# A GeGLU feed-forward kernel by seven-product blocks: one plain tile at the head instead of two, seventeen gate products before the first half of x

## The chip, the cores and the metric

The kernel runs on one core of one Trainium2 chip. The metric is the device time of one execution in microseconds (us). Nine runs of the kernel before lie between 274.5 and 275.85 us, with a median of 275.36 us.

## What is computed

```python
B, S, D, F = 32, 32, 1024, 3584        # 1024 tokens
def reference(x, w_gate, w_up, w_down):
    return (_gelu(x @ w_gate) * (x @ w_up)) @ w_down    # all bf16, gelu with tanh
```

## The kernel before, in words

**Two layers.** The first layer makes g = gelu(x·w_gate)·(x·w_up), transposed, in 28 tiles of 128 columns of F (FT = 28). The second multiplies g by w_down and stores the result. The change touches the first layer only, above all its first 30 us.

**Seven products instead of eight.** For one tile of F, the two weight matrices and the two halves of D (rows of x transposed) and of the tokens form a 2x2 by 2x2 block product. The blocks of weights are a11 and a12 (gate, front and rear half of D) and a21 and a22 (up, front and rear). The blocks of x are b11, b21 (tokens 0 to 511, front and rear half of D) and b12, b22 (tokens 512 to 1023). Each block product is KD = 4 matmuls of 128x128 by 128x512. Done plainly a tile takes eight of them for its two matrices and two halves of the tokens (32 matmuls). Done by the Strassen-Winograd scheme it takes seven (28 matmuls), at the price of sums of blocks:

- sums of weights, one set for each tile: s1 = a21 + a22, s2 = s1 - a11, s4 = a12 - s2, s3 = a11 - a21 (`sums`, lines 161 to 171; they are made for a chunk of two tiles at once);
- sums of x, made once: t1 = b12 - b11 (L331), t2 = b22 - t1 (L336), t3 = b22 - b12 (L379), t4 = b21 - t2 (L381), and the copy b22r of b22 (L337).

The seven products are P1 = a11·b11 and P2 = a12·b21, which are in bf16, and s1·t1, s2·t2, s4·b22, s3·t3 and a22·t4, whose operands are 32 bits wide (fp32r).

**Chunks and the loop.** Tiles go in chunks of FC = 2. The two tiles of chunk 0 are done plainly while x and its sums are not there yet (`plain`, L250 to L258, for both halves of the tokens). The loop at L387 handles chunks 1 to 13. For the tiles of one chunk, TensorE does s1·t1 into a bank `psc`, which ScalarE copies out (`sn5`), then s2·t2 on top of P1 in `psa` (copied out as `sn2`), then the last product a22·t4 of the chunk before, then s4·b22 on top of `psc`. VectorE adds `sn2` and `psc` (`added`, L348 to L351), and ScalarE makes `h1` = gelu of that and then the copy `a22r` (L177), which is the last read of that tile's up-weights. Then come P2, where it is still to be made, P1 of the next chunk (`first_product`, L358), and s3·t3.

**P2 ahead.** P2 needs only b21, the quarter of x that is loaded first. For the first NAHEAD = 10 tiles after chunk 0 (tiles 2 to 11) it is made ahead (`product_ahead`, L283) from `a12_ahead`, loaded as three groups of KB = 4, 4 and 2 tiles, and copied to `ahead` by ScalarE and VectorE. `first_product` adds it to P1 later (a read of `psa` and of `ahead` on VectorE).

**Who makes the sums of weights.** VectorE makes them for chunk 1, GpSimd for chunks 2 to 13, one chunk before they are used. At L383 a copy of one column of t4 into `ident` on GpSimd holds GpSimd's queue until t4 is there:

```python
        begun = [first_product(FC + fl, p1[fl]) for fl in range(FC)]
        tt(t3, b22, b12, SUB)
        next(chunk1)
        tt(t4, b21, t2, SUB)
        nc.gpsimd.tensor_copy(ident[:, :1], t4[:, 0, :1])
```

**Order and buffers.** The schedule is manual: each engine runs its instructions in the order in which the program names them, and waits on semaphores. Nearly all loads are issued from SyncE's queue in the order written. x comes through DMA transposes (`load_xT`), apart from the first quarter of b21, which TensorE transposes. Eight PSUM banks have tags: A has four, B two and C two; a bank is given out again in turn (`acc`, L104). Up-weights have two buffers (`wu`), gate-weights three (`wg`).

Of the kernel before, what the change touches and what calls it, by code (L numbers as in the profile page):

```python
# [13 lines left out]
def kernel(  # L14
# [20 lines left out]
    nc = tc.nc  # L35
    P = nc.NUM_PARTITIONS
    fp32 = mybir.dt.float32
# [9 lines left out]
    NB = 512  # L47
# [4 lines left out]
    NCH = FT // FC  # L52
    NAHEAD = 10
# [21 lines left out]

    def g_tiles(name, dtype, cols):

        return [
            gpool.tile(
                [P, k1 - k0, cols],  # L80
                dtype,
                name=name,
                tag=f"{name[:2]}{k1 - k0}",
                bufs=2,
            )
            for k0, k1 in batches
        ]

    g_lo = g_tiles("lo", bf16, N)

    def by_batch(tiles):
        def at(k):
            b = next(i for i, (k0, k1) in enumerate(batches) if k < k1)
            return tiles[b][:, k - batches[b][0], :]

        return at

    def g_of(ft):
        k = ft % HF
        return by_batch(g_lo if ft < HF else g_hi)(k)  # L100
# [15 lines left out]
    def x_rows(dt, nb):  # L116
        return ((b11, b12), (b21, b22))[dt // KD][nb][:, dt % KD, :]


    ahead = [  # L120
        gpool.tile([P, n, NB], fp32, name="ahead", tag=f"hi{n}", bufs=2) for n in (KB, KB, QF - KB)
    ]
    assert 2 * KB < NAHEAD <= KB + QF
# [7 lines left out]
    def load_w(eng, ci, which, d0, d1):  # L131
        f0 = ci * FC * P
        src = (wg_r, wu_r)[which]
        eng.dma_start(out=w_tiles[ci, which][:, d0:d1, :], in_=src[:, d0:d1, f0 : f0 + FC * P])

    def load_w_all(ci, which):

        alloc_w(ci, which)
        if ci < NCH - 2:
            load_w(nc.sync, ci, which, 0, KD if which == 0 and is_ahead(ci) else DT)  # L140
            return


        for d0 in (0, KD):
            load_w(nc.sync, ci, which, d0, d0 + KD)

    def is_ahead(ci):
        return 0 < ci and (ci + 1) * FC <= FC + NAHEAD

    def quads(ci, fl=None):  # L150
        cols = slice(None) if fl is None else slice(fl * P, (fl + 1) * P)
        wg, wu = w_tiles[ci, 0], w_tiles[ci, 1]
        a12 = wg[:, KD:, cols]
        if is_ahead(ci):
            i, j = divmod((ci - 1) * FC, KB)
            a12 = a12_ahead[i][:, :, j * P : (j + FC) * P][:, :, cols]
        return wg[:, :KD, cols], a12, wu[:, :KD, cols], wu[:, KD:, cols]
# [3 lines left out]
    def sums(ci, eng):  # L161

        a11, a12, a21, a22 = quads(ci)
        s1, s2, s4, s3 = (
            spool.tile([P, KD, FC * P], f32r, name=n, tag=n) for n in ("s1", "s2", "s4", "s3")
        )
        s_tiles[ci] = (s1, s2, s3, s4)
        yield eng.tensor_tensor(s1, a21, a22, ADD)  # L168
        yield eng.tensor_tensor(s2, s1, a11, SUB)  # L169
        yield eng.tensor_tensor(s4, a12, s2, SUB)  # L170
        yield eng.tensor_tensor(s3, a11, a21, SUB)  # L171

    a22rs = {}

    def a22r_of(ft):
        t = spool.tile([P, KD, P], f32r, name="a22r", tag="a22r", bufs=2)
        nc.scalar.copy(t, quads(*divmod(ft, FC))[3])  # L177
        a22rs[ft] = t
# [10 lines left out]
    with tc.manual_schedule():  # L189
# [12 lines left out]
        def load_ahead(i, k0, k1, eng=nc.sync):  # L202
            f0, n = FC + i * KB, min(KB, NAHEAD - i * KB)
            eng.dma_start(
                out=a12_ahead[i][:, k0:k1, : n * P],
                in_=wg_r[:, KD + k0 : KD + k1, f0 * P : (f0 + n) * P],
            )

        def load_w0(eng, d0, d1):
            for which in (0, 1):  # L210
                load_w(eng, 0, which, d0, d1)
# [10 lines left out]
        for which, eng in enumerate((nc.sync, nc.scalar)):  # L222
            load_w(eng, 0, which, KD, KD + KQ)
        load_xT(0, KD + KQ, DT)
        load_ahead(0, KQ, KD)
        load_w0(nc.sync, KD + KQ, DT)
        load_ahead(1, 0, KD)
        load_xT(0, 0, KD)
        load_w0(nc.sync, 0, KD)
        load_xT(1, 0, KD)  # L230
        load_xT(1, KD, DT)

# [17 lines left out]
        def plain(ps, which, fl, nb, d0, d1, first=0, last=DT - 1):  # L250
            for dt in range(d0, d1):
                nc.tensor.matmul(  # L252
                    ps,
                    lhsT=w_tiles[0, which][:, dt, fl * P : (fl + 1) * P],
                    rhs=x_rows(dt, nb),
                    start=(dt == first),
                    stop=(dt == last),
                )  # L258
# [6 lines left out]
        def plain_out(ft, nb, h, up):  # L265
            tt(g_of(ft)[:, nb * NB : (nb + 1) * NB], h, up, MUL)
# [12 lines left out]
        def ahead_of(ft):  # L279
            i, j = divmod(ft - FC, KB)  # L280
            return ahead[i][:, j, :]

# [10 lines left out]


        ps = [acc(t) for t in "CCAA"]

        def plain0(tok0, d0, d1):
            for which in (0, 1):
                for dt in range(d0, d1):
                    for fl in range(FC):  # L300
                        plain(tok0[fl][which], which, fl, 0, dt, dt + 1, KD, KD - 1)
# [9 lines left out]
        tok0 = [(acc("A"), acc("B")) for _ in range(FC)]  # L311
        plain0(tok0, KD, KD + KQ)
        for j, copy in enumerate((nc.scalar.copy, nc.vector.tensor_copy) * 2):
            product_ahead(ps[j], 0, j, KQ)
            copy(ahead[0][:, j, :], ps[j])
        plain0(tok0, KD + KQ, DT)
        a12_ahead.append(xpool.tile([P, KD, (NAHEAD - 2 * KB) * P], bf16, name="a12b"))
        load_w_all(1, 1)
        load_w_all(1, 0)
        load_ahead(2, 0, KD)  # L320
        load_w_all(2, 0)
        for j, tag in enumerate("CCAA"):
            ps = acc(tag)
            product_ahead(ps, 1, j)
            (nc.scalar.copy, nc.vector.tensor_copy)[j % 2](ahead[1][:, j, :], ps)
        for fl in range(FC):
            for which in (0, 1):
                plain(tok0[fl][which], which, fl, 0, 0, KD, KD, KD - 1)
            plain_out(fl, 0, gelu(tok0[fl][0], "h0", 4), tok0[fl][1])
            if fl == 0:  # L330
                tt(t1, b12, b11, SUB)  # L331
        tok1 = [(acc("A"), acc("B")) for _ in range(FC)]
        for fl in range(FC):
            for which in (0, 1):
                plain(tok1[fl][which], which, fl, 1, 0, KD)
        tt(t2, b22, t1, SUB)  # L336
        nc.scalar.copy(b22r, b22)  # L337
        chunk1 = sums(1, nc.vector)
        for _ in range(3):
            next(chunk1)  # L340
        for fl in range(FC):
            for which in (0, 1):
                plain(tok1[fl][which], which, fl, 1, KD, DT)
            tok1[fl] = gelu(tok1[fl][0], "h0", 4), tok1[fl][1]
        load_w_all(2, 1)
# [12 lines left out]
        def first_product(ft, psa=None):  # L358
            if psa is None:
                psa = acc("A")  # L360
                prod(psa, quads(*divmod(ft, FC))[0], b11, True)
            if ft < FC + NAHEAD:
                return psa, gelu(added(ahead_of(ft), psa), "h0", 4)
            return psa, snap(psa, "sn1")
# [6 lines left out]
        p1 = [acc("A") for _ in range(FC)]  # L371
        for fl in range(FC):
            prod(p1[fl], quads(1, fl)[0], b11, True)
        for j, tag in enumerate("CC"):
            ps = acc(tag)
            product_ahead(ps, 2, j)
            nc.scalar.copy(ahead[2][:, j, :], ps)  # L377
        begun = [first_product(FC + fl, p1[fl]) for fl in range(FC)]
        tt(t3, b22, b12, SUB)  # L379
        next(chunk1)  # L380
        tt(t4, b21, t2, SUB)  # L381

        nc.gpsimd.tensor_copy(ident[:, :1], t4[:, 0, :1])  # L383
        for fl in range(FC):
            plain_out(fl, 1, *tok1[fl])
        open_fts = []
        for ci in range(1, NCH):  # L387
            fts = range(ci * FC, (ci + 1) * FC)
            if fts[0] == HF:
                g_hi = g_tiles("hi", bf16, N)  # L390
# [5 lines left out]
            s1, s2, s3, s4 = ([s[:, :, fl * P : (fl + 1) * P] for fl in range(FC)] for s in s_tiles[ci])  # L396
# [3 lines left out]
            for fl in range(FC):  # L400
                prod(psc[fl], s1[fl], t1, True)
                sn5.append(snap(psc[fl], "sn5"))
            for fl in range(FC):
                prod(psa[fl], s2[fl], t2, False)
                sn2.append(snap(psa[fl], "sn2"))
# [9 lines left out]
            if fts[0] < FC + NAHEAD:  # L415
                h0 = first
            else:
                for fl in range(FC):
                    psb = acc("B")
                    prod(psb, quads(ci, fl)[1], b21, True)  # L420
                    h0.append(gelu(added(first[fl], psb), "h0", 4))
            begun = [first_product(ft + FC) for ft in fts] if ci + 1 < NCH else []
# [193 lines left out]
```

## Time and profile before

| what | value |
|---|---|
| median of nine runs | 275.36 us (274.5 to 275.85) |
| profiled execution, its own time | 275.64 us |
| span of that execution | 273.9 us |
| TensorE (PE) busy | 268.8 us, 98% of the span |
| VectorE (DVE), ScalarE (ACT), GpSimd (POOL) busy | 195.5, 111.1, 107.4 us |
| read from HBM | 29.62 MB |

Times below are microseconds from the span's start. In a timeline a row gives the start, the time taken, the engine, the line of the kernel, the operation, output<-input with the shapes, and in brackets the idle time of the engine before it with what ended it. PEld is TensorE's weight load, which overlaps its matmuls; SPq is SyncE's queue of DMA issues. A matmul's row lasts longer than the distance to the next, since matmuls are pipelined.

### The profile page before, as it was taken

The numbers are of one execution on the slowest core, as the hardware profiler recorded it, in microseconds if no ns is written. First come the engines' busy times: TensorE is split into PE (matmuls) and PEld (weight loads), VectorE is DVE, ScalarE is ACT, GpSimd is POOL, SyncE is SP. The second block draws the span as 40 slices with busy tenths as digits, with TensorE's granted clock in tenths as the row PEclk, the third lists the DMA queues.
The fourth block names the chain that finished last, engine by engine and source line by source line (L and its number), as shares of the span: only waits on it lengthen the run. The fifth ranks groups of instructions, "written<-read, shape, count | busy, mean of one in ns | idle before, by whom it ended". The sixth has DMA issues, their size and how long they took to land.

```text
span 273.9 us, 3350 instructions
## 1 busy us (share of the span) xinstructions
PE 268.8 (98%) x1190; PEld 189.4 (69%) x1206; DVE 195.5 (71%) x196; ACT 111.1 (41%) x181; POOL 107.4 (39%) x55
## 2 busy tenths in 40 slices
PE   8999999999999999999999999999999999999995
PEld 4444677877778676776868686755447888888883
DVE  1259996879856676766666556568989999999611
ACT  1162654543653646455553636430200032962001
POOL 1000099998797794949576675000000000000000
PEclk9999999999999999999999999999999999999999
DMA  7993412404505415050504280003992245786202
GB/s 193 283 246 86 115 54 61 117 26 130 151 6 152 125 31 154 0 153 0 156 20 134 71 273 4 0 2 112 352 333 87 78 145 199 245 262 223 78 0 78
DMA packets 53841, 33.77 MB, mean 123 GB/s; under 512 B 9792, under 2 KB 53824, under 8 KB 53824
## 3 DMA queue, kind: packets, MB, share of 16 engines
q1 hardware_dynamic: 50304, 31.00, 38.7%
q10 hardware_dynamic: 3520, 2.56, 2.9%
q8 instruction: 9, 0.15, 0.3%
q14 instruction: 8, 0.07, 0.1%
HBM read 29.62 MB, written 2.10 MB: 116 GB/s over the span
## 4 chain that ended last, share of the span: by engine, by line
PE 98%; issue 0%; ACT 0%; DVE 0%
PE psA L270 34%; PE psA L446 18%; PE psC L270 17%; PE psC L446 7%; PE psB L446 7%; PE psB L270 5%; PE psB L252 3%; PE psA L252 2%; PE psC L285 2%; PE psA L285 1%; PE psA L235 1%; PE tp L243 0%; ACT o_sb L586 0%; DVE b L246 0%
## 5 line engine op out<-in xcount | busy, mean ns | idle before, releaser
L270 PE MATMUL psA<-t,s 128*128 128x512 f32 x208 | 54.1, 402 | 0.0
L262 ACT ACTIVATE h<-c 128x512 bf16<-128x512 f32 x52 | 31.6, 627 | 36.9 <-DVE c L350 36.9
L270 PEld LDWEIGHTS psA<-t,s 128*128 128x128 f32 x208 | 39.1, 188 | 9.2
L168 POOL TENSOR_TENSOR s<-wu 128x1024 fp32r<-128x1024 bf16 x12 | 26.5, 2206 | 25.0 <-DMA wu<-in_w_up_dram 21.5
L350 DVE TENSOR_TENSOR c<-sn,psA 128x512 f32<-128x512 f32 x26 | 17.8, 683 | 16.7 <-PE psA L270 16.7
L270 PEld LDWEIGHTS <-wg 128*128 128x128 bf16 x168 | 15.4, 98 | 20.1 <-issue 3.4
L169 POOL TENSOR_TENSOR s<-s,wg 128x1024 fp32r<-128x1024 f32 x12 | 27.8, 2314 | 0.9
L171 POOL TENSOR_TENSOR s<-wg,wu 128x1024 fp32r<-128x1024 bf16 x12 | 26.6, 2213 | 0.0
L355 ACT COPY sn<-psA 128x512 f32<-128x512 f32 x42 | 23.6, 585 | 7.0 <-PE psA L270 6.9
L270 PE MATMUL psA<-t,a22r 128*128 128x512 f32 x104 | 25.9, 391 | 0.0
L270 PE MATMUL psC<-t,s 128*128 128x512 f32 x104 | 25.8, 390 | 0.0
L355 ACT COPY sn<-psC 128x512 f32<-128x512 f32 x26 | 15.2, 589 | 26.2 <-PE psC L270 22.4
L270 PE MATMUL psC<-b22r,s 128*128 128x512 f32 x104 | 25.7, 389 | 0.0
L270 PE MATMUL psA<-b,wg 128*128 128x512 bf16 x100 | 24.1, 379 | 0.2
L270 PEld LDWEIGHTS psC<-t,s 128*128 128x128 f32 x104 | 19.4, 188 | 4.4 <-ACT ahead L377 0.3
L270 PEld LDWEIGHTS psA<-t,a22r 128*128 128x128 f32 x104 | 19.5, 188 | 4.1
L270 PEld LDWEIGHTS psC<-b22r,s 128*128 128x128 f32 x104 | 19.5, 188 | 4.0
L350 DVE TENSOR_TENSOR c<-sn,psC 128x512 f32<-128x512 f32 x26 | 17.6, 686 | 5.0 <-PE psC L270 5.0
L369 DVE TENSOR_TENSOR hi<-h,psA 128x512 bf16<-128x512 bf16 x14 | 9.6, 688 | 14.6 <-PE psA L270 14.6
L425 DVE TENSOR_TENSOR lo<-c,h 128x512 bf16<-128x512 f32 x12 | 19.2, 1597 | 0.6
L170 POOL TENSOR_TENSOR s<-wg,s 128x1024 fp32r<-128x1024 bf16 x8 | 17.3, 2158 | 0.6
L489 ACT COPY snb<-psC 128x512 f32<-128x512 f32 x4 | 2.1, 589 | 36.5 <-PE psC L446 36.5
(94 smaller groups left out, 412.3 us busy)
## 6 DMA issues: line engine op xcount, KB each, us to landing
wdb<-in_w_down_dram SPq DMA_DIRECT2D x12, 512.0 KB, 4.8
wu<-in_w_up_dram SPq DMA_DIRECT2D x11, 512.0 KB, 3.9
wdb<-in_w_down_dram SPq DMA_DIRECT2D x12, 384.0 KB, 4.7
wg<-in_w_gate_dram SPq DMA_DIRECT2D x6, 512.0 KB, 5.1
wg<-in_w_gate_dram SPq DMA_DIRECT2D x10, 256.0 KB, 4.3
v<-in_w_down_dram SPq DMA_DIRECT2D x4, 512.0 KB, 7.6
out_dram<-o_sb ACTq DMA_DIRECT2D x16, 128.0 KB, 1.7
v<-in_w_down_dram SPq DMA_DIRECT2D x4, 384.0 KB, 7.9
```

The source lines that it names most:

```text
L168: yield eng.tensor_tensor(s1, a21, a22, ADD)
L169: yield eng.tensor_tensor(s2, s1, a11, SUB)
L170: yield eng.tensor_tensor(s4, a12, s2, SUB)
L171: yield eng.tensor_tensor(s3, a11, a21, SUB)
L252: nc.tensor.matmul(ps, lhsT=w_tiles[0, which][:, dt, fl * P : (fl + 1) * P], rhs=x_rows(dt, nb), start=(dt == first), stop=(dt == last),)
L262: nc.scalar.activation(h, src, ACT.Gelu_apprx_tanh)
L270: nc.tensor.matmul(ps, lhsT=lhs[:, k, :], rhs=rhs[:, k, :], start=(start and k == 0), stop=(k == KD - 1), skip_group_check=True,)
L350: tt(t, s, ps, ADD)
L355: nc.scalar.copy(t, ps)
L369: tt(g_of(ft)[:, :NB], h0, psa, MUL)
L425: tt(g_of(ft)[:, NB:], added(sn5[fl], psa[fl]), h1[fl], MUL)
L446: nc.tensor.matmul(banks[m], lhsT=lhs(k)[:, m * P : (m + 1) * P], rhs=rhs(k), start=(start and k == 0), stop=(k == HF - 1), skip_group_che ...
```

## The change

- **Chunks.** Only tile 0 is done plainly. Chunk 0 of the loop is now tile 1 alone, done by seven products; chunks 1 to 13 are as before. NCH stays 14.
- **P2 ahead.** 17 tiles instead of 10: tile 1 (from chunk 0's own weights) and four full groups, tiles 2 to 17. The last two groups lie in buffers of `s2` and `s4` that are reused later, so the a12 weights of tiles 10 to 17 are loaded a second time with their chunk (`a12_stays` is true for tiles 2 to 9 only).
- **Loads.** The four groups and all of chunk 0's weights come before b11, b12 and b22.
- **Order at the head.** Groups 1, 2 and 3 of P2 ahead, then tile 0's front half for tokens 0 to 511, its front half for the other tokens, P1 of tile 1, and tile 0's rear half for the other tokens. VectorE makes the sums of chunk 0 (128x512 each) ahead of t1; GpSimd makes those of chunks 1 to 13.
- **The hold on GpSimd** is on t2 instead of t4, and stands before t4.
- Buffers of `ahead` and of g are shared in another way, and of all later loads of weights only the last chunk's gate-weights still come in two halves (before: gate and up of the last two chunks).

```diff
+    chunks = [range(1, FC)] + [range(f0, f0 + FC) for f0 in range(FC, FT, FC)]
+    NCH = len(chunks)
+    NAHEAD = 17
...
-        if ci < NCH - 2:
-            load_w(nc.sync, ci, which, 0, KD if which == 0 and is_ahead(ci) else DT)
+        if (ci, which) != (NCH - 1, 0):
+            load_w(nc.sync, ci, which, 0, KD if which == 0 and a12_stays(ci) else DT)
...
+        a12_ahead += [spool.tile([P, KD, KB * P], bf16, name="a12b", tag=t) for t in ("s2", "s4")]
         load_xT(0, KD + KQ, DT)
         load_ahead(0, KQ, KD)
         load_w0(nc.sync, KD + KQ, DT)
-        load_ahead(1, 0, KD)
+        for i in (1, 2):
+            load_ahead(i, 0, KQ)
+            load_ahead(i, KQ, KD)
+        load_w0(nc.sync, 0, KD)
+        load_ahead(3, 0, KD)
         load_xT(0, 0, KD)
-        load_w0(nc.sync, 0, KD)
         load_xT(1, 0, KD)
         load_xT(1, KD, DT)
+        for which in (1, 0):
+            load_w_all(1, which)
...
+        both = (nc.scalar.copy, nc.vector.tensor_copy)
+        tok0 = (acc("B"), acc("B"))
+        p2_1 = acc("A")
...
+        rear0(KD, KD + KQ)
+        for j in range(KB):
             product_ahead(ps[j], 0, j, KQ)
...
+        rear0(KD + KQ, DT)
+        nc.scalar.copy(ahead_at[0], p2_1)
+        group_ahead(1, "CCAA", both)
+        group_ahead(2, "CCAA", both)
+        for _ in sums(0, nc.vector):
+            pass
+        group_ahead(3, "CCAA")
+        for which in (0, 1):
+            plain(tok0[which], which, 0, 0, KD, KD, KD - 1)
+        tt(t1, b12, b11, SUB)
+        plain_out(0, gelu(tok0[0], "h0", 4), tok0[1])
+        tok1 = (acc("C"), acc("A"))
+        for which in (0, 1):
+            plain(tok1[which], which, 1, 0, KD)
+        p1 = acc("A")
+        prod(p1, quads(0, 0)[0], b11, True)
+        for which in (0, 1):
+            plain(tok1[which], which, 1, KD, DT)
+        nc.scalar.copy(b22r, b22)
         tt(t2, b22, t1, SUB)
...
+        begun = [first_product(1, p1)]
+        tok1 = gelu(tok1[0], "h0", 4), tok1[1]
         tt(t3, b22, b12, SUB)
-        next(chunk1)
+
+        nc.gpsimd.tensor_copy(ident[:, :1], t2[:, 0, :1])
         tt(t4, b21, t2, SUB)
-
-        nc.gpsimd.tensor_copy(ident[:, :1], t4[:, 0, :1])
-        for fl in range(FC):
-            plain_out(fl, 1, *tok1[fl])
+        plain_out(1, *tok1)
         open_fts = []
-        for ci in range(1, NCH):
-            fts = range(ci * FC, (ci + 1) * FC)
+        for ci in range(NCH):
+            fts = chunks[ci]
```

In the changed kernel `rear0` does, for the given quarter of D, tile 0's gate and up matmuls for tokens 0 to 511 and tile 1's P2; `group_ahead(i, ...)` does the four products of group i and copies them out.

## The prediction

> **What bounds the kernel now.** The first page says it at once: TensorE is busy nearly all the time, and the chain that ended last is TensorE.
>
> ```profile
> PE 268.8 (98%) x1190; PEld 189.4 (69%) x1206; DVE 195.5 (71%) x196; ACT 111.1 (41%) x181; POOL 107.4 (39%) x55
> ...
> PE 98%; issue 0%; ACT 0%; DVE 0%
> ```
>
> So time comes only from fewer matmuls or from a wait of TensorE, and in the stage that is changed there is none to win: the chain of waits in order of time runs from 4.1 us on without a gap over 0.07 us. It also gives the price of a matmul:
>
> ```profile
> 24.72 0.86 PE psA L252 x4
> ...
> 31.82 1.81 PE psA L270 x8
> ```
>
> A bf16 matmul of 512 columns takes 0.216 us (0.865/4), one with 32-bit operands 0.227 (1.814/8). I then read VectorE's timeline from 28 to 37 us and GpSimd's whole one, since the change moves what these two do there.
>
> ```profile
> 28.81 2.29 DVE L379 TENSOR_TENSOR t<-b,b 128x2048 fp32r<-128x2048 bf16 x1
> 31.02 1.22 DVE L171 TENSOR_TENSOR s<-wg,wu 128x1024 fp32r<-128x1024 bf16 x1
> 32.15 2.29 DVE L381 TENSOR_TENSOR t<-b,t 128x2048 fp32r<-128x2048 bf16 x1
> ```
>
> ```profile
> 34.60 0.19 POOL L383 CAST ident<-t 128x1 bf16<-128x1 f32 x1 [33.30 <-PE psC L270]
> 34.81 2.13 POOL L168 TENSOR_TENSOR s<-wu 128x1024 fp32r<-128x1024 bf16 x1
> ```
>
> Up to 34.4 us VectorE makes t1 to t4 and four sums with GpSimd idle: each 128x2048 step starts 2.2 us before the next. GpSimd's first sum begins 0.37 us after t4's end (34.44). What happens when both work is seen later, in VectorE's timeline and in GpSimd's at the same moment:
>
> ```profile
> 60.60 2.51 DVE L425 TENSOR_TENSOR lo<-c,h 128x512 bf16<-128x512 f32 x1
> 63.04 0.67 DVE L350 TENSOR_TENSOR c<-sn,psA 128x512 f32<-128x512 f32 x1
> 63.75 2.67 DVE L425 TENSOR_TENSOR lo<-c,h 128x512 bf16<-128x512 f32 x1
> ```
>
> ```profile
> 60.41 2.16 POOL L171 TENSOR_TENSOR s<-wg,wu 128x1024 fp32r<-128x1024 bf16 x1
> 63.72 2.14 POOL L168 TENSOR_TENSOR s<-wu 128x1024 fp32r<-128x1024 bf16 x1 [1.15 <-DMA wu<-in_w_up_dram]
> 65.94 2.48 POOL L169 TENSOR_TENSOR s<-s,wg 128x1024 fp32r<-128x1024 f32 x1
> ```
>
> L425 takes 0.69 us where GpSimd is idle. Here both its inputs lie in SBUF and it ends 0.54 us after GpSimd's sum ends (62.57, 65.86): it stands still until the sum is through. GpSimd's next sum is then late in its turn (2.48 for 2.15). L350, which reads one input from PSUM, is not touched (0.67 to 0.69 beside GpSimd).
>
> **The change, part by part.** The sum is made against the profiled execution (275.64 us, span 273.9), which lies 0.28 above the median; a difference is then put on the median.
>
> *Matmuls.* Tile 1 goes from 32 bf16 matmuls to 8 in bf16 and 20 in 32 bits: -24 x 0.2163 + 20 x 0.2267 = -5.19 + 4.53 = **-0.66 us**, all on the path. The P2 of tiles 12 to 17 only moves from the loop to the head. Their evictions change from a snapshot and an addition to a copy and an addition (0.59 and 0.69 us either way), on engines with idle time in every later chunk: nothing.
>
> *Loads.* Twelve issues stand before b11 now, at about 0.5 us each on SyncE: the last plain one would be issued by some 9 us. The groups 2 and 3 put 1024 KB ahead of b22, and the weights of chunk 0 and all groups come ahead of b11. Before, 4096 KB landed by 18.3 us (b22: issued at 14.0, 4.3 to landing; b12 16.3, b11 11.8), from about 2.0: 257 GB/s. With the 1.05 MB more, b22 lands at 18.3 + 4.1 = 22.4, b12 at 20.4, b11 near 17.9 (estimates from these rows). Who needs them: TensorE from 7.29, where the half-width products end, does 6 + 8 + 6 + 3 x 16 = 68 matmuls before it touches b11, so until 22.0; b12 at 23.7; b22 after 96 matmuls less 8, at 26.3. Groups 1, 2 and 3 are needed at 11.6, 15.1 and 18.5 and land at about 10, 12 and 16. So the loads are hidden by the products ahead; if the cover failed, each us of b22 after 25.3 would cost one. The second load of a12 for tiles 10 to 17 (1024 KB) lies in the loop, where the DMA engines are 18 to 39% busy: nothing.
>
> *VectorE up to t2.* The last copy of group 2 starts when its product ends, 18.7, so the sums of chunk 0 run from 19.3 (128x512 each, 0.61 apart by the pairs of L350) to 21.8, t1 to 24.07. ScalarE copies group 3 until 22.8, loads the table for gelu (1.28 us, as at 15.86 before) and ends gelu at 24.7; tile 0's product with it takes VectorE to 25.4, t2 to 27.6. Then `added` for tile 1, to 28.2. TensorE starts chunk 0 after 96 matmuls, 7.29 + 20.77 = 28.06, does s1·t1 (t1 is there) and wants t2 and that `added` at 28.97. Cover: 0.8 us. Between s1·t1 and s4·b22 there is now one product (0.91) instead of four, and ScalarE has two gelus (28.2 to 29.3) before the copy of `psc`: it ends at 29.9, wanted at 29.88. I take +0.05, with 0 to 0.4 as bounds.
>
> *VectorE after t2, the new wait.* The hold on GpSimd now ends with t2, so its first sum starts at 27.6 + 0.37 = 28.0 if the up-weights of chunk 1 are there (before they landed at 23.0, 4.7 after b22; now with one transfer less beside them, some 4 after 22.4). t3 would start at 28.1, with both inputs in SBUF. By the rows above it waits for the sum (30.1) and ends at 32.2; then GpSimd's second sum has been waiting and runs to 34.2; t4 ends at 36.3. Behind t4 in VectorE's order stand tile 0's other product (to 36.9) and `added` of `sn2` and `psc` (to 37.5). Who waits: bank C is given out in turn, so the second s1·t1 of chunk 1 goes into the bank that this `added` reads. TensorE arrives there after s4·b22 (29.9 to 30.8), P1 of tiles 2 and 3 (to 32.55; s3·t3 just finds t3), s3·t3 (33.46) and the first s1·t1: 34.37. Wait: 37.55 - 34.37 = **+3.2 us**. Without GpSimd t3 and t4 would end at 32.6 and that `added` at 33.85, before it is wanted. The trace of before shows no two SBUF-only steps of VectorE in a row against GpSimd; the bounds are none delayed (0) and both delayed by a sum (3.2). I take both, since in the rows above each side gets its turn after one instruction of the other; with t3 delayed alone it is 35.6 - 34.4 = 1.2.
>
> After that wait there is room. GpSimd's sums for chunk 1 end near 41; s2, wanted at 38.5, ended at 34.2, and s4, wanted at 41.2, ends at 38.5. Chunk 2's up-weights wait for `a22r` of tile 1 (38.7), land at 42.8 by the 4.0 us of before, and their s1 (45.0) is wanted at 46.5.
>
> *Sum.* -0.66 + 0.05 + 3.2 = +2.6: the median goes to 278.0.
>
> Two rules of the Trainium skill bear on this. The page "SBUF — State Buffer", section "SBUF: two separate sides", says that GpSimd and a VectorE instruction with two SBUF inputs share one port pair as an exclusive lock for a whole instruction; it agrees with the L425 rows, speaks against moving the hold from t4 to t2, and a proportional sharing, which it rules out, would give about half the delay. The page "TensorE: Matmul & The Clock Gate", section "Part 1: The HAM clock gate (the "warmup" mystery)", says that an idle window of about 3.4 us halves TensorE's clock; a wait of 3.2 would just stay below it, and no row here shows an idle TensorE of that length.
>
> **The rivals.**
> *One delay only (25%).* Either VectorE keeps its turn for t4, or the up-weights of chunk 1 land after 28.1, so that t3 goes first and only t4 waits for one sum. For it: the second case needs the weights only 1.5 us later than I reckon. Against: the turns seen in the L425 rows. Time: the wait is 1.2 to 1.4, the sum +0.6 to +0.8: 276.1.
> *No wait, faster (20%).* t3 and t4 lose under 0.5 us to GpSimd, so that `added` ends at 34.4 or before, and the matmuls decide: -0.66 + 0.05 = -0.6, with ScalarE's 0.4 -0.3: 274.75 to 275.1. It decides if t4 ends before 33.1. For it: its rows are 2.29 us when GpSimd is idle, and TensorE would then find each operand. Against: every L425 row that meets a sum.
> *x or the clock (8%).* Transposed loads come at under 225 GB/s, so that 5.24 MB are not there by 25.3, or TensorE's clock falls in the wait. For it: in the head, up to 6.8 us, matmuls are 0.43 us apart instead of 0.216, so a half rate exists; 4 us of it would cost 2. Against: 3 us of margin. Time: 280.
>
> **How the numbers follow.** Both delayed 47%, 278.0 (277.4 to 278.7 with the bounds of ScalarE and of t2's end); the others as above. The range from 274.8 to 279.0 leaves out the last rival and the lower part of the faster one. A difference within 0.2% (0.55 us) is about what a measurement of this kernel can tell from none. Faster: 12 of the 20% of the second rival. The same: the other 8 and 5 of the 25% of the first. Slower: 47 + 20 + 8 = 75%.
>
> **What would show it.** Right: TensorE's matmul count falls by 4; t3 and t4 rows of over 4 us instead of 2.29 beside GpSimd's first two sums; a TensorE gap of about 3 us near 34 to 38 us, ended by VectorE's `added`; no gap before 28 us; 30.7 MB read. Wrong: t3 and t4 near 2.3 us, or a gap that a DMA of x ends before 27 us.

## The result and the profile after

The changed kernel takes 279.58 us in the median of 10 runs (277.45 to 280.55), the kernel before 275.29 (31 runs): a ratio of 1.0142, with a 95% interval from 1.0121 to 1.0163 (the ratio goes by the averages, 279.26 over 275.35; the medians differ by 4.29 us). It is slower by about 4 us. The forecast was slower by 2.6 (278.0), and its range ended at 279.0.

The profiled execution took 279.89 us, 4.25 more than that of the kernel before. The first page, with the rows that answer to those shown before:

```profile
span 278.1 us, 3359 instructions
PE 270.1 (97%) x1186; PEld 191.7 (69%) x1202; DVE 196.9 (71%) x201; ACT 112.8 (41%) x183; POOL 118.3 (43%) x59
...
HBM read 30.67 MB, written 2.10 MB: 118 GB/s over the span
...
PE 96%; issue 2%; DVE 1%; ACT 0%; DVEq 0%
```

TensorE has four matmuls fewer (x1186 for x1190; its weight loads, x1202 for x1206, say the same), the second load of a12 is there (30.67 MB), and TensorE no longer carries the whole chain. VectorE's timeline around t2 (L357), t3 (L385) and t4 (L388), and then GpSimd's:

```profile
25.34 2.28 DVE L357 TENSOR_TENSOR t<-b,t 128x2048 fp32r<-128x2048 bf16 x1
27.54 0.68 DVE L362 TENSOR_TENSOR c<-ahead,psA 128x512 f32<-128x512 f32 x1
28.14 4.15 DVE L385 TENSOR_TENSOR t<-b,b 128x2048 fp32r<-128x2048 bf16 x1
32.21 4.22 DVE L388 TENSOR_TENSOR t<-b,t 128x2048 fp32r<-128x2048 bf16 x1
36.36 0.68 DVE L279 TENSOR_TENSOR lo<-h,psA 128x512 bf16<-128x512 bf16 x1
36.95 0.67 DVE L362 TENSOR_TENSOR c<-sn,psC 128x512 f32<-128x512 f32 x1
```

```profile
27.79 0.19 POOL L387 CAST ident<-t 128x1 bf16<-128x1 f32 x1 [26.48 <-DVE t L357]
27.99 2.14 POOL L171 TENSOR_TENSOR s<-wu 128x1024 fp32r<-128x1024 bf16 x1
30.21 4.07 POOL L172 TENSOR_TENSOR s<-s,wg 128x1024 fp32r<-128x1024 f32 x1
34.36 4.07 POOL L173 TENSOR_TENSOR s<-a12a,s 128x1024 fp32r<-128x1024 bf16 x1
```

The two queues take turns, one instruction each: s1 until 30.1, t3 until 32.3, s2 until 34.3, t4 until 36.4, s4 after it. Rows of 2.1 to 2.3 us become rows of 4.1 to 4.2, about half of each spent standing still; s1, which began first, keeps its 2.14, and the addition from PSUM (L362) is not lengthened. What TensorE makes of it, in its timeline:

```profile
32.49 1.28 PE L283 MATMUL psA<-t,s 128*128 128x512 f32 x4
33.61 1.08 PE L283 MATMUL psC<-t,s 128*128 128x512 f32 x4
37.68 2.07 PE L283 MATMUL psC<-t,s 128*128 128x512 f32 x4 [2.99 <-DVE c L362]
39.55 2.62 PE L283 MATMUL psA<-t,s 128*128 128x512 f32 x8
```

The second s1·t1 of chunk 1 could have started at 33.61 + 0.91 = 34.52 and started at 37.68, 3.16 us later. (The bracket says 2.99, since it counts from the end of the last row, and a row lasts about 0.16 us beyond the moment when the next matmul could start. So the time lost is that much more than a bracket says, here and below.) Behind it four matmuls take 2.07 us instead of 1.08, and that is not in the forecast. The table of windows has the reason in the number ahead of the DMA share, TensorE's granted clock (PEclk, 1.00 is full speed):

```profile
core 0: us, PE busy (x) PEld busy (x) DVE busy (x) ACT busy (x) POOL busy (x), PEclk, DMA share, GB/s
37.00:38.00 1.00, 0.32 (x1) 0.32 (x2) 1.00 (x3) 0.34 (x1) 1.00 (x1) 0.73 0.00 0
38.00:39.00 1.00, 1.00 (x3) 0.81 (x3) 1.00 (x3) 1.00 (x3) 1.00 (x2) 0.50 0.00 0
39.00:40.00 1.00, 1.00 (x4) 0.71 (x4) 0.96 (x2) 1.00 (x3) 1.00 (x1) 0.50 0.05 11
40.00:41.00 1.00, 1.00 (x4) 0.81 (x3) 1.00 (x1) 0.81 (x2) 0.53 (x1) 0.56 0.81 218
41.00:42.00 1.00, 1.00 (x6) 0.80 (x5) 0.08 (x1) 0.59 (x1) 0.00 (x0) 1.00 1.15 345
```

The clock is at one half from 37.5 to 40.9. TensorE has work again from 37.68, so that costs 0.16 + 0.50 + 0.50 + 0.44 = 1.60 us of full-speed time. In the chain of waits the second layer starts 4.27 us later than before; first the row of before, then that of after:

```profile
181.11 1.74 PE psC L446 x8
```

```profile
185.38 1.74 PE psC L448 x8
```

Of these 4.27 us, -0.66 (matmuls) + 3.16 (the wait) + 1.60 (the clock) account for 4.10. Another 0.04 is a later head (the first full-width product starts at 7.33, before at 7.29); 0.13 are left, and the run with both orders joined says more on them.

Not every execution loses the clock. Seven of the ten had a mean clock of 0.987 to 0.994 and took 279.43 to 280.55 us (the two at 0.987, about twice the loss of 0.994, took 280.46 and 280.55); three had 0.998 or 1.0 and took 277.45, 277.85 and 277.89, which is the forecast's case.

### The profile page after: what moved, and what is told of

Its sections match the earlier page's. It is cut to its first block, busy times and chain, and to the rows that moved or that the text cites. A ratio compares the mean times of both kernels' runs of the same rounds, so it can differ in the third digit from the quotient of the medians.

```text
span 278.1 us, 3359 instructions
## 1 busy us (share of the span) xinstructions
PE 270.1 (97%) x1186; PEld 191.7 (69%) x1202; DVE 196.9 (71%) x201; ACT 112.8 (41%) x183; POOL 118.3 (43%) x59
## 3 DMA queue, kind: packets, MB, share of 16 engines
HBM read 30.67 MB, written 2.10 MB: 118 GB/s over the span
## 4 chain that ended last, share of the span: by engine, by line
PE 96%; issue 2%; DVE 1%; ACT 0%; DVEq 0%
PE psA L283 34%; PE psA L448 18%; PE psC L283 18%; PE psC L448 7%; PE psB L448 7%; PE psB L283 3%; PE psC L294 3%; PE psA L294 3%; PE psB L265 1%; PE psA L248 1%; PE psC L265 1%; PE psA L265 1%; DVE t L388 1%; DVE lo L279 0%; PE tp L256 0%
## 5 line engine op out<-in xcount | busy, mean ns | idle before, releaser
L283 PE MATMUL psA<-t,s 128*128 128x512 f32 x216 | 57.1, 406 | 0.0
L275 ACT ACTIVATE h<-c 128x512 bf16<-128x512 f32 x54 | 33.1, 628 | 44.9 <-DVE c L362 44.9
L283 PEld LDWEIGHTS psA<-t,s 128*128 128x128 f32 x216 | 41.2, 191 | 9.9
L171 POOL TENSOR_TENSOR s<-wu 128x1024 fp32r<-128x1024 bf16 x13 | 28.9, 2220 | 25.2 <-DMA wu<-in_w_up_dram 14.8
L172 POOL TENSOR_TENSOR s<-s,wg 128x1024 fp32r<-128x1024 f32 x13 | 30.8, 2373 | 1.0
L283 PE MATMUL psC<-t,s 128*128 128x512 f32 x108 | 28.1, 401 | 3.0 <-DVE c L362 3.0
L174 POOL TENSOR_TENSOR s<-wg,wu 128x1024 fp32r<-128x1024 bf16 x13 | 28.3, 2179 | 0.0
L362 DVE TENSOR_TENSOR c<-sn,psA 128x512 f32<-128x512 f32 x27 | 18.4, 682 | 11.7 <-PE psA L283 11.7
L283 PEld LDWEIGHTS <-wg 128*128 128x128 bf16 x148 | 13.4, 98 | 17.8 <-issue 3.7
L367 ACT COPY sn<-psA 128x512 f32<-128x512 f32 x37 | 21.1, 586 | 7.6 <-PE psA L283 7.5
L362 DVE TENSOR_TENSOR c<-sn,psC 128x512 f32<-128x512 f32 x27 | 18.6, 687 | 6.1 <-PE psC L283 6.0
L173 POOL TENSOR_TENSOR s<-wg,s 128x1024 fp32r<-128x1024 bf16 x9 | 19.4, 2155 | 0.7
```

The lines of the kernel that those rows point to most:

```text
L275: nc.scalar.activation(h, src, ACT.Gelu_apprx_tanh)
L283: nc.tensor.matmul(ps, lhsT=lhs[:, k, :], rhs=rhs[:, k, :], start=(start and k == 0), stop=(k == KD - 1), skip_group_check=True,)
L362: tt(t, s, ps, ADD)
L367: nc.scalar.copy(t, ps)
```

## The experiments

Lines are those of the changed kernel, times those of each run's own profile; the head of an execution can lie up to 0.9 us earlier or later on that scale, so waits are compared and not moments. The kernel before ran at 274.94 us beside the runs with the hold on t4, with twelve matmuls in the gap, with t4 later and with GpSimd's sums of chunk 0; at 275.03 beside the changed kernel again, four matmuls, another bank and both orders joined; at 275.29 and 275.24 beside the last two.

**The hold on t4 again.**

```diff
-        nc.gpsimd.tensor_copy(ident[:, :1], t2[:, 0, :1])
         tt(t4, b21, t2, SUB)
+        nc.gpsimd.tensor_copy(ident[:, :1], t4[:, 0, :1])
```

> The changed kernel with one part undone: the hold on GpSimd is on t4 again. Theory (GpSimd's first sums hold up t3 and t4, and VectorE's addition behind them holds up TensorE): t3 and t4 take 2.29 us each again, t4 ends at 32.6 and the addition of sn2 and psc is no longer what TensorE waits for. In its place TensorE waits for GpSimd itself: its first sum for chunk 1 starts at 33.0 and ends at 35.1, wanted at 33.5 (1.6 us), the second ends at 37.3, wanted at 37.0 (0.3). Two short waits of 1.9 us in all instead of one of 3.2, too short for the clock to fall: 275.3 - 0.6 + 1.9 = 276.6 us, clock 1.0. Rival (the wait comes from VectorE's own amount of work at the head, not from GpSimd): VectorE's rows and the wait stay, about 279.5 us.

Measured: 276.63 us, ratio 1.0061 (1.0049 to 1.0073). t3 and t4 are back at 2.28, and TensorE's largest wait is for GpSimd:

```profile
34.77 2.12 PE L283 MATMUL psC<-t,s 128*128 128x512 f32 x8 [1.42 <-POOL s L171]
```

The theory holds, the rival falls: with GpSimd out of the way, VectorE's own work is in time. With the hold on t2, GpSimd's first sum is in time and TensorE waits longer for VectorE instead; with the hold on t4 the change is still slower than the kernel before, by 0.6%.

**Work for TensorE in the gap.**

```diff
                 prod(psc[fl], s1[fl], t1, True)
+                if ci == 1 and fl == 0:
+                    spare = acc("B")
+                    for _ in range(12):
+                        nc.tensor.matmul(spare, lhsT=ones_w, rhs=ones_m, start=True, stop=True)
```

> The changed kernel with 12 matmuls on constants into an unused bank (2.6 us of TensorE's work that nobody reads) between the two s1.t1 of chunk 1, where TensorE waited from 34.6 to 37.7. Theory (the time above the forecast is the clock that fell in that wait, half rate from 37.3 to 40.9): the wait for VectorE's addition still ends at 37.6, the matmuls behind it come 0.227 apart at once, granted clock 1.0 in every run, 275.3 - 0.6 + 3.2 = 277.8 us. Rival (the clock falls for another reason, or the 1.6 us are lost elsewhere): 279.5 us, clock 0.99, as without the filling; or, if the filling costs TensorE time, over 280.

Measured: 278.06 us (277.64 to 278.27), ratio 1.0109 (1.0096 to 1.0122), clock 0.998 to 1.0 in all four executions. VectorE is as late as before (t3 and t4 take 4.15 and 4.22), but the wait that TensorE sees is short and what follows it is at full speed:

```profile
36.85 1.21 PE L283 MATMUL psC<-t,s 128*128 128x512 f32 x4 [0.39 <-DVE c L362]
37.90 2.01 PE L283 MATMUL psA<-t,s 128*128 128x512 f32 x8
```

So 2.6 us of useless matmuls make the changed kernel 1.5 us faster in the median (1.2 when each is set against the kernel before that ran beside it). That shows the clock as the cause of what the forecast lacked.

**The changed kernel again, and four matmuls in the gap instead of twelve** (the same edit with `range(4)`).

> The changed kernel as it is, on the same chip as the next three. Theory (a wait of about 3 us, after which the clock falls in most executions and not in all): two groups of executions, some near 277.5 to 277.9 us with clock 1.0 and more near 279.5 with clock 0.99. Rival (the fall of the clock belongs to the chip of the first runs): all near 277.7, clock 1.0.

> The changed kernel with 4 instead of 12 matmuls on constants in the gap (0.9 us of work that nobody reads; TensorE is left without work for about 2.2 us). Theory (the clock falls only where the idle time comes close to 3 us): clock 1.0 in nearly all executions, 277.8 us, as with 12. Rival (any idle time of over 1 us, or the wait as such, can halve the clock): part of the executions near 279.5 us.

Measured: the changed kernel 279.91 us (279.79 to 280.18), ratio 1.0170 (1.0156 to 1.0184), the clock at 0.992 to 0.994 in all four executions. With four matmuls 278.23 us, ratio 1.0107 (1.0089 to 1.0125); four executions at 277.77 to 278.3 with clock 0.998 to 1.0, one at 279.0 with 0.994. The two rows of the wait:

```profile
37.63 2.08 PE L283 MATMUL psC<-t,s 128*128 128x512 f32 x4 [2.99 <-DVE c L362]
```

```profile
37.03 1.20 PE L283 MATMUL psC<-t,s 128*128 128x512 f32 x4 [2.11 <-DVE c L362]
```

The fall belongs neither to the chip nor to every wait: where the profile has 2.99 us of idle TensorE, the clock fell in 11 of 14 executions over both sets, with 2.11 us in 1 of 5, with 1.42 us (hold on t4) in none of 5. The idle times are those of the profiled executions; the one that fell with four matmuls has no profile, so whether its idle time was longer or the limit is not sharp stays open.

**Another bank for tile 1's psc.**

```diff
-            psc = [acc("C") for _ in fts]
+            psc = [acc("C" if ci else "B") for _ in fts]
```

> The changed kernel with tile 1's psc in a bank of tag B, so that the second s1.t1 of chunk 1 finds its bank free. Theory (TensorE waits for VectorE's queue behind t3 and t4; the bank is only the place where it meets it): that matmul runs at its time, and TensorE waits 0.9 us later, at s2.t2 of tile 2, for the addition behind t4 (ends 38.2 on the scale of the changed kernel); the end of the wait moves the product behind it, so 0.3 us are won and no more: 277.5 us with clock 1.0, 279.2 where it falls. Rival (giving out bank C in turn is the cause): the wait is gone, 274.7 to 275.2 us.

Measured: 279.15 us (278.05 to 279.46), ratio 1.0135 (1.0116 to 1.0153); one execution of five kept its clock, at 278.05.

```profile
32.95 2.00 PE L283 MATMUL psC<-t,s 128*128 128x512 f32 x8
37.72 2.92 PE L283 MATMUL psA<-t,s 128*128 128x512 f32 x8 [2.77 <-DVE c L362]
```

Both s1·t1 now run in one go, and the wait stands one product later, at s2·t2, for the next addition behind t4. The bank was only where TensorE met VectorE's queue. The clock fell later here than in the changed kernel: at 38.7, 1.0 us after TensorE had started again (1.00 from 38.0 to 38.7, 0.51 from 38.7 to 39.7), where there it fell at 37.5, 0.2 us before TensorE started again. It stayed at one half for 3.4 us in both. So the idle stretch alone does not set the moment of the fall; what else does, and why some executions escape, no run here shows.

**t4 later in VectorE's order.** The hold stays on t2.

```diff
-        tt(t4, b21, t2, SUB)
-        plain_out(1, *tok1)
...
             begun = [first_product(ft) for ft in chunks[ci + 1]] if ci + 1 < NCH else []
+            if ci == 0:
+                tt(t4, b21, t2, SUB)
...
+            if ci == 0:
+                plain_out(1, *tok1)
             open_fts = list(zip(fts, psa, h0))
```

> The changed kernel with VectorE's order altered and the hold on GpSimd left on t2: t4 stands behind the additions of tile 1's sn2 and of tiles 2 and 3, tile 0's second output at the end of chunk 0. t3 still waits for GpSimd's sum and ends at 32.3, t4 now runs at about 34.3 to 36.4. Theory: the bank of the second s1.t1 is free at 32.9, before it is wanted; what is late next is GpSimd's third sum (ends 38.5, wanted 38.0): 0.5 us. 275.3 - 0.6 + 0.5 = 275.2 us, clock 1.0. Rival (the wait is in the amount of work of VectorE and GpSimd, whatever the order): a wait of some 3 us appears at s2.t2 or at the last product of tile 1, 278 to 279.5 us.

Measured: 275.09 us (274.69 to 275.47), ratio 1.0004 (0.9995 to 1.0013). TensorE's one marked wait between 8 and 44 us is that for GpSimd's third sum:

```profile
37.68 2.14 PE L283 MATMUL psC<-b22r,s 128*128 128x512 f32 x8 [0.18 <-POOL s L173]
```

That product could have started at 37.29 (36.38 and four matmuls), so 0.39 us are lost there, near the 0.5 expected. The place of two instructions in one queue is worth over 4 us here, clock included. t3 still stands still for 1.9 us (4.15), and nobody waits for it.

**GpSimd makes the sums of chunk 0.** It is idle until 28 us, so VectorE can begin t1 earlier. t2 and t3 follow at once, the hold is on t4.

```diff
-        for _ in sums(0, nc.vector):
+        for _ in sums(0, nc.gpsimd):
...
         tt(t1, b12, b11, SUB)
-        plain_out(0, gelu(tok0[0], "h0", 4), tok0[1])
+        tt(t2, b22, t1, SUB)
+        tt(t3, b22, b12, SUB)
+        h_0 = gelu(tok0[0], "h0", 4)
...
         tt(t4, b21, t2, SUB)
+        nc.gpsimd.tensor_copy(ident[:, :1], t4[:, 0, :1])
+        plain_out(0, h_0, tok0[1])
         plain_out(1, *tok1)
```

> A version that follows from the theory: GpSimd, idle until 28 us, makes the sums of chunk 0, so VectorE begins t1 at 19.4 and makes t2 and t3 at once, then the addition for tile 1, t4 (ends about 29.5) and the two outputs of tile 0; the hold on GpSimd is on t4. GpSimd's sums for chunk 1 then end at 31.9, 34.1, 36.2 and are wanted at 33.5, 35.3, 38.0. Theory: no wait of TensorE, only the 0.6 us of the saved matmuls are left: 274.7 us, clock 1.0, ratio to before 0.998. Rival (x lands too late for t1 to start earlier, b12 after 21 us): t1 to t4 move by less than 1.5 us, GpSimd's first sum is late by about 1 us, 275.5 to 276 us.

Measured: 275.61 us (274.86 to 276.7), ratio 1.0023 (1.0011 to 1.0034): a miss. VectorE's timeline, then TensorE's:

```profile
21.29 2.29 DVE L347 TENSOR_TENSOR t<-b,b 128x2048 fp32r<-128x2048 bf16 x1 [2.02 <-DMA b<-in_x_dram]
```

```profile
30.48 1.17 PE L283 MATMUL psC<-b22r,s 128*128 128x512 f32 x4 [0.45 <-ACT sn L368]
```

As the rival had it, x came too late in this execution: t1 waited for b12 until 21.3 and so moved by 0.7 us only. (In the profile of the next run t1 starts at 19.33 without that wait, so b12 does not come at the same time in every execution.) t3 then stood ahead of the addition for tile 1, ScalarE's gelu and its copy of `psc` came late behind that, and s4·b22 waited.

**Both orders joined.** GpSimd makes the sums of chunk 0, t2 directly follows t1, the addition for tile 1 stands ahead of t3, t4 is late as above, and the hold is on t2.

> The two orders joined: GpSimd makes the sums of chunk 0, VectorE makes t1 and t2 as soon as b12 and b22 are there, then tile 0's first output, the addition for tile 1, t3, the additions of chunk 0, and only then t4; tile 0's second output comes last; the hold on GpSimd is on t2. In the last run of this kind t3 stood ahead of the addition for tile 1 and ScalarE's copy of psc was 0.5 us late; here it is not. Theory: t2 ends about 1.5 us earlier than in the changed kernel, GpSimd's sums for chunk 1 end 1.5 us earlier and in time even with t3 and t4 between them, and TensorE waits for nothing over 0.2 us: the saved matmuls alone, 0.6 us under the kernel before, ratio 0.998. Rival (x is now what t1 waits for, b12 after 22 us): t2 no earlier than in the changed kernel and 0.3 to 0.5 us of waiting for GpSimd's third sum, ratio 1.000.

Measured: 275.04 us (274.17 to 275.46), ratio 0.9994 (0.9983 to 1.0006). In its profiled execution TensorE waits for nothing from 12 to 46 us, and its second layer starts at 180.58, 0.53 before that of the kernel before. The two executions compare well, since full-width products start at 7.30 and 7.29. So 0.53 of the reckoned 0.66 us is there, and -0.53 + 3.16 + 1.60 + 0.04 is the 4.27 of the changed kernel; the missing 0.13 has no row of its own. The median shows nothing of the gain. In that execution t2 still waits 1.46 us for b22, and TensorE started relatively late. Whether a wait appears in the executions that start early stays open.

**x ahead of the last group.**

```diff
-        load_ahead(3, 0, KD)
         load_xT(0, 0, KD)
         load_xT(1, 0, KD)
         load_xT(1, KD, DT)
+        load_ahead(3, 0, KD)
...
-        group_ahead(3, "CCAA")
...
         begun = [first_product(1, p1)]
         tok1 = gelu(tok1[0], "h0", 4), tok1[1]
+        group_ahead(3, "CCBB")
```

The sums of chunk 0 are on GpSimd, t2 follows t1, and the hold is on t4.

> A version that puts x ahead of the last group: the loads of b11, b12 and b22 stand before group 3's weights, and TensorE does tile 0's products and P1 of tile 1 before group 3 (into banks C and B), so that 3.5 us of products lie between the last use of b22 by TensorE and chunk 0. GpSimd makes the sums of chunk 0; VectorE makes t1 to t4 without GpSimd, whose hold is on t4 again. Theory: x lands some 2 us earlier, t2 ends near 24, t4 near 29.5; GpSimd's sums for chunk 1 end at 32, 34.2 and 36.3 and are wanted at 33.5, 35.3 and 38 (0.8 earlier in executions whose clock rises early); nothing waits: only the 0.6 us of the saved matmuls, ratio 0.998, 274.4 to 274.6 us. Rival (the last kernel without a wait of TensorE in its profile was no faster than the kernel before, so the 0.66 us of matmuls are not there to be had): ratio 1.000, 275.0 us.

Measured: 275.62 us (275.3 to 276.1), ratio 1.0003 (0.9986 to 1.0021). The rival's number, but TensorE's timeline shows a wait that I had put in with the banks:

```profile
26.43 1.02 PE L294 MATMUL psC<-b,a12b 128*128 128x512 bf16 x4 [0.74 <-ACT h L275]
```

**The same with group 3 in banks B, B, C, C** (`group_ahead(3, "BBCC")`).

> The version with x ahead of the last group, with one thing altered: group 3 goes into banks B, B, C, C instead of C, C, B, B, since in the last run its second product waited 0.74 us for bank C, which ScalarE's gelu of tile 0 still had to read. Theory (each wait in the profile counts in full, and the saved matmuls too): no wait of TensorE from 8 us to the end of the first layer, 0.74 us less than the last run, ratio 0.998, 0.5 to 0.6 us under the kernel before. Rival (the saved matmuls are not there to be had, or another wait comes): ratio 1.000.

Measured: 274.88 us (274.44 to 275.26), ratio 0.9986 (0.9977 to 0.9995), and 0.74 us less than the run before, on another chip (0.69 when each is set against the kernel before that ran beside it): about the wait that was taken out. In TensorE's timeline of this profile no wait of a matmul is marked between 4.4 and 50 us, but not all of it is gone:

```profile
25.70 1.89 PE L294 MATMUL psC<-b,a12b 128*128 128x512 bf16 x8
27.72 1.16 PE L283 MATMUL psC<-t,s 128*128 128x512 f32 x4
28.72 1.09 PE L283 MATMUL psA<-t,s 128*128 128x512 f32 x4
```

From 25.70 to 28.72 are 3.02 us, where 8 x 0.2163 + 4 x 0.2267 = 2.64 would do: 0.38 us are still lost at s1·t1. s1·t1 goes into a bank that group 3 has just used, and ScalarE's two copies out of the banks C run from 26.97 to 28.22; that they are the cause is likely and not shown. This version is faster than both kernels, by 0.14% against the kernel before. Its 0.36 us are less than the 0.66 of the matmuls; the interval (0.14 to 0.63 us) stops just short of it and holds the 0.53 of the run with both orders joined.

## Why the prediction was right or wrong

The sign and the mechanism of the wait were right, the size was not: 278.0 forecast, 279.58 measured, outside the range. What was missing is a second effect of that wait, the fall of TensorE's clock.

- **Matmuls, -0.66:** four fewer in the profile, and the sign was right. The size is a little large: 0.53 us came out in the one profile without a marked wait that compares well with before, 0.36 in the median of the last experiment. With 0.66 the account of the profiled execution leaves 0.13 us over.
- **ScalarE's copy, +0.05:** it ended at 29.85, and s4·b22 started 0.92 after the product before it (0.91 at the price): no wait to speak of.
- **Loads hidden:** right. TensorE has no gap from 4.3 to 28 us, and t1 starts straight behind the sums of chunk 0. The margin was thinner than reckoned for VectorE: with the sums out of the way, t1 waited for b12 in one execution (until 21.3, where I had estimated 20.4) and not in another.
- **VectorE up to t2:** t2 ended at 27.62, forecast 27.6.
- **The wait behind t3 and t4:** right in each step. t3 ended at 32.29 (32.2), t4 at 36.43 (36.3), the addition at 37.62 (37.5); the wait was 3.16 us (3.2). The step that the trace of before could not show, who goes first when VectorE has two such instructions in a row, is settled by the rows above: they alternate.
- **No further wait behind it:** right; chunk 2 began without one.
- **The clock: the step that failed.** The sum had no term for it; it stood in the last rival, at 8% and 280 us, and the range stopped short of that rival. Measured: the clock fell in 7 of 10 executions, and in the profiled one that cost 1.60 us. The row that I had weighed was the head's half rate up to 6.8 us; it says that a half rate exists and how much it costs, and nothing about the idle time that brings it on. For that I leaned on the page "TensorE: Matmul & The Clock Gate" of the Trainium skill, section "Part 1: The HAM clock gate (the "warmup" mystery)", whose idle window is about 3.4 us, and read a wait of 3.2 as just below it. The runs decide against that reading: with 2.99 us of idle time in the profile the clock fell in 11 of 14 executions, with 2.11 us in 1 of 5. The same section has the full clock come back after about 3.4 us of sustained work; here it came back 3.4 us after the fall (37.5 to 40.9), 3.2 of them with work. A wait so close to a limit deserved a chance near one half, and with 1.6 us added the likeliest time would have been 279.6.
- **The page "SBUF — State Buffer"**, section "SBUF: two separate sides", on the exclusive lock agrees with the rows: t3 (4.15 us) stands still for the whole of s1 that is left (until 30.13) and then takes 2.16, about its usual time, and s1 keeps its 2.14. The prediction's remark that a proportional sharing would give about half the delay does not follow: with each side at half speed t3 would end near 32.5 too (an estimate from 2.28 and 2.14). What tells the two apart is s1's row, which sharing would have stretched.

## What to carry to other kernels

When an engine is handed work earlier, look at which instructions of its neighbour then run beside it, and what is queued behind those: here two of VectorE's instructions lost 1.9 us each to GpSimd, and it was their place ahead of three small additions that cost 3.2 us; moving t4 behind these (and an output of tile 0 to the end) gave nearly all of it back. In this kernel a wait of TensorE of 2 us or more is not priced by its length alone, since the clock may fall with it; a few matmuls on constants in the gap are a cheap way to find out. A gain of half a microsecond from four matmuls is hidden by any wait of that length, so each wait in the timeline is worth naming before the next version is made, and the distance from product to product is worth reckoning where no wait is marked.

## What the hardware showed that was not expected

- TensorE's granted clock fell to one half for 3.4 us in 11 of 14 executions where the profile has 2.99 us of idle time, in 4 of 5 with 2.77 us (another bank), in 1 of 5 with 2.11 us, in none with 1.42 us. With 2.77 us it fell 1.0 us after the work had started again.
- Two VectorE instructions in a row with both inputs in SBUF do not keep GpSimd out: each side gets one instruction in turn (4.15 and 4.22 us on VectorE, 4.07 and 4.07 on GpSimd, for 2.29 and 2.15 alone).
